# Adding the two halves of the attention result on TensorE, inside the transpose, for the first two tiles of each layer, with a new order of the whole program

## Chip, cores and metric

One core of one Trainium2 chip. The metric is the device time of one execution in microseconds. Times are medians over the runs of one kernel. Every changed kernel is compared with runs of the kernel before on the same chip in the same rounds.

## The reference

A residual stack with two identical layers over 2048 rows of 512 columns (bf16). Each layer is a linear attention with learned feature maps, then a gated MLP with ReLU gate.

```python
# per layer, 32 heads of 16
q, k, v = split(layernorm(x) @ wqkv)
phi = lambda y: concat(softmax(y @ w_phi), softmax(-(y @ w_phi)))    # 16 -> 32 features
kv, z = phi(k)^T v,  sum over rows of phi(k)
o = (phi(q) @ kv) / (phi(q) @ z + 1e-6)
x = x + o @ wo
g, u = layernorm(x) @ W_gate, layernorm(x) @ W_up      # 512 -> 1376
x = x + ((g * (g > 0)) * u) @ W_down
# twice: attention, MLP, attention, MLP
```

The keys' sums `kv` and `z` run over all 2048 rows. So all of a layer's keys must be done before any query can be used. At that point, twice in the program, TensorE has little other work, and the first tiles' attention stands alone on the way to the first MLP matmul.

## The kernel before

The rows are 16 tiles of 128. The kernel is a list of operations, each with an engine, a cost, dependencies, and a buffer pool. A planner in the kernel simulates the engines with these costs and fixes the order in which instructions are issued on each engine. Two tables steer it: `DUE`, one priority for each operation, and `PLACE`, one bit for each copy that could run on ScalarE or VectorE. Both were evidently tuned for this one program.

The softmax of `phi(q)` has two halves (`+` and `-`). Their exponentials `Eq` are multiplied by a matrix `R` (built from `kv` and `z`); numerators and denominators come out of PSUM as `N` and `DS`. VectorE makes the factors `w` and scales both halves in one multiplication to `pr`. Then the halves are added:

```python
# attend(): one tile
a = op("DVE", dve(1024, 2), ... out=pr.t[:], in0=N.t[:], in1=w...broadcast, op=Alu.mult, name="pr")
a = op("DVE", dve(512, 2), due, lambda: nc.vector.tensor_tensor(
    out=o.t[:]..., in0=pr.t[:, 0], in1=pr.t[:, 1], op=Alu.add), [a], [o], [pr], name="o", port=True)
a = turn(o, lambda: oT.t[:], how, due, a, [oT], [], "oT")
a = op("PE", mm(4, 512), ... lhsT=oT.t[:, b, :], rhs=wo[:, b, :], name="proj")        # o @ wo
a = op("DVE", dve(512), ... out=x, in0=x, in1=yp.t[:], op=Alu.add, name="resA")       # residual
# ... stats, centring (xn), turn to xnTB, then the MLP's matmuls on wgu

# turn(): a tile transposed
if how == "SP":                      # by DMA: tiles 2 to 15
    return op("SP", ... dma_start_transpose(out=dst(), in_=src.t[:]))
ps = Buf(p_b)                        # on TensorE: tiles 0 and 1 of each layer ("early")
a = op("PE", mm(4, 128), due, lambda: [nc.tensor.matmul(
    ps.t[:, b * P:(b + 1) * P], lhsT=src.t[:, b * P:(b + 1) * P], rhs=ident[:], start=True, stop=True)
    for b in range(NB)], [after, c_id], [ps], [src], name=name)
return evac(how, ...)                # copy PSUM -> SBUF, on ScalarE or VectorE as PLACE says

# the end: the order of the planner is issued; fillers on zeros go in where the plan has TensorE idle, in the start
order = arrange(ops)
for o in order:
    if o.eng == "PE": ... idle(max(0, int((o.start - free - 150) / FILL))) ...
    o.emit()
```

The softmax here doesn't subtract the row's maximum and nothing guards it: scores larger than these inputs give would overflow.

Of the kernel before, what the change touches and what calls it, by code (L numbers as in the profile page):

```python
# [10 lines left out]
H = 32  # L11
# [25 lines left out]
class Op:  # L37
# [3 lines left out]
    def __init__(self, eng, cost, due, emit, deps=(), takes=(), uses=(), name="", move=0, port=False,  # L41
                 follow=(), alt=None):
        self.eng, (self.occ, self.lat) = eng, cost
        self.due, self.emit, self.name, self.move, self.port = due, emit, name, move, int(port)
        self.deps = [d for d in deps if d is not None]
        self.follow = [d for d in follow if d is not None]
        self.takes, self.uses = list(takes), list(uses)
        self.then, self.behind, self.alt, self.twin = [], [], alt, None
# [162 lines left out]
DVE0 = (85, 170)  # L211
RLN, REXP = ((150, 265), (203, 318)), ((145, 262), (198, 315))
# [13 lines left out]
class K:  # L226
# [9 lines left out]
    "0000000100000001001000000000100000000000010001111000011000011001110000000000011010000001001111001100"  # L236
    "0100000110110100010000011011100101111100101001111000111010100001001101101100100110011001110011001001"
    "1111001110100000000011100010100100000101001110100111000101101010101000101010111001010111100010110100"
# [3 lines left out]
PHI0 = ["POOL", "POOL", "DVE"] * 5 + ["BOTH"]  # L242
PAIRN, PAIRK = 4, T
# [5 lines left out]
    76719491, 69466873, 69464194, 55720479, 42085309, 40348612, 33593703, 42085031, 50665322, 33594228, 56086954,  # L249
    58486545, 100334641, 61163217, 49431745, 41251988, 69056115, 9741064, 80414090, 80414120, 53308772, 80413780,  # L250
    106435297, 49852457, 80414139, 49848882, 56526831, 56526817, 69547873, 53741705, 49852168, 66481170, 68934086,
    55660918, 50246487, 32405931, 57594884, 55662420, 50058741, 44536605, 58281570, 3, 22509044, 49850622, 49848858,
    69548291, 69463783, 49850611, 55051722, 76716792, 0, 55324383, 47430106, 32690380, 59187722, 60929485, 45084743,
    53725584, 55713647, 55727277, 54655971, 49923445, 50246438, 55324400, 55324343, 35442704, 55802924, 35441651,
    55161101, 53685522, 51682019, 33202876, 47809082, 52941970, 53687226, 55701298, 55711066, 55655645, 44505335,
    54950229, 47610086, 55322999, 47811927, 35002194, 55588705, 62960580, 55157588, 53726567, 47768162, 55269518,
    47767416, 55571188, 53304664, 55688755, 55180830, 55625721, 50380932, 40642846, 40645264, 47809620, 55323699,
    57680173, 55268245, 54520833, 53558741, 55098763, 55683455, 55732950, 55683459, 55697315, 55770465, 52825634,
    55713412, 55710946, 55506275, 54950156, 35001190, 54949680, 34999890, 59085355, 62960363, 54948116, 55748897,
    55646532, 56083290, 53268545, 59116845, 55619542, 55763775, 53310977, 55774953, 55764998, 55740543, 52826475,  # L260
    55685321, 52784010, 55711099, 55519531, 56373630, 50382939, 52826205, 52825598, 55778163, 55771090, 55181433,
    55768958, 55684488, 55709355, 55684978, 55522442, 55648291, 55646610, 55689548, 54948629, 55098862, 47766546,
    54948487, 56010726, 55697946, 55693442, 55936025, 53268542, 44506128, 55691384, 55769572, 55545075, 55409199,
    55692897, 55662797, 55667892, 55709660, 55713749, 55700261, 55690361, 55371927, 55946741, 55947245, 55372043,
    55396376, 55760995, 55660101, 55570763, 55708913, 55708943, 50191721, 55658940, 55569634, 55658937, 55655528,
    52824974, 54566163, 55181604, 56093099, 55623488, 55927755, 55388217, 55697886, 55645404, 55667208, 55921043,
    55691484, 55685094, 55623151, 55652318, 55396329, 55703531, 55760168, 55699699, 55388529, 55623507, 55651900,
    55396324, 56045911, 55709610, 55623568, 55048436, 55709159, 56660851, 55240452, 55696214, 55974927, 55693988,
    55741153, 55693228, 55396401, 55665438, 55487833, 55388179, 55703473, 55388150, 55305368, 57292002, 55522439,
    55570606, 54081536, 55694997, 57095763, 45526601, 45175404, 54082167, 55710694, 56661198, 55697150, 54522450,  # L270
    47668141, 45175447, 49709693, 50191138, 48930643, 51185210, 41476757, 41476428, 56663182, 55710691, 55700162,
    55966393, 55623154, 55694078, 55418211, 55667889, 55662695, 50622534, 54522884, 55759099, 54522768, 55305365,
    53814510, 54207260, 51926549, 56731158, 22533505, 86923532, 49054124, 54577294, 50454445, 56663443, 26743223,
    64933030, 26742771, 41476589, 77848357, 55701636, 46564931, 86922882, 76909815, 56851302, 56665549, 49600025,
    49129654, 50619771, 50620709, 50622827, 56301309, 54209613, 56114277, 54821759, 49333488, 51487502, 52263956,
    39762113, 19221682, 41476432, 41476507, 40958443, 51486441, 50279390, 16984712, 37300570, 50960427, 49597502,
    35848215, 39760598, 24648533, 41476504, 55699989, 55704953, 48137801, 50278843, 46562185, 37300567, 49597307,
    49597499, 35844120, 55705982, 39761347, 49335617, 38759704, 49337568, 39761346, 55750849, 56154495, 33592791,
    56153063, 32405860, 51221336, 55803472, 55693594, 55803225, 55321390, 55802697, 53688156, 49597175, 49597541,
    49597913, 49596963, 58672801, 49543902, 49597043, 49596659, 55778023, 55771093, 55123240, 55776845, 55771414,  # L280
    55772175, 53557771, 53310277, 53304643, 44505573, 53310550, 55124938, 56045945, 55661057, 55711116, 55624256,
    55667825, 55396537, 56736587, 57094903, 54082104, 57408271, 54209459, 57094884, 55827685, 46563699, 56440267,
    55828521, 55702687, 46562936, 55705068, 48140907, 48140902, 56553271, 55701218, 55705063, 55720810, 56440270,
    48141651, 55702429, 55696714, 55697995, 59129153, 55703718, 55704014, 55827014, 48137480, 46562610, 30585230,
    58655341, 49560287, 21530914, 52917937, 47182136, 30584484, 55701037, 46563696, 52917833, 41444195, 41443940,
    47181589, 47181495, 41443844, 55700488, 53497782, 38496984, 56130655, 55690360, 55704606, 53137802, 55693769,
    55703325, 53137820, 55692042, 50947124, 55405040, 50987789, 41443966, 41414378, 55870566, 52917866, 55300343,
    55700485, 52129878, 61996903, 62505784, 55697736, 53137801, 55550154, 55700626, 55740601, 55699572, 55699299,
    55704914, 55699024, 58344346, 62506293, 50451565, 49470778, 53245447, 53278134, 49336219, 55704076, 55886670,
    55697360, 53497785, 55550159, 55699902, 55700360, 55698793, 55698582, 52841760, 55869605, 55108122, 54090734,  # L290
    55300268, 62506063, 62660753, 62506806, 55705573, 49344780, 55886105, 55700933, 49470866, 56146496, 55700624,
    55692773, 55692770, 55701615, 55740476, 49312541, 55752952, 49765942, 55886212, 55430767, 55238713, 55977103,
    55691820, 55688056, 47612654, 55699803, 55700555, 55697628, 55700835, 55741749, 55700975, 55702709, 55575076,
    55692884, 53991858, 53991972, 53990466, 54779534, 53853809, 54779664, 55691422, 55704463, 55620232, 55701498,
    55691964, 55738452, 55702685, 56001882, 55694740, 55702008, 55709199, 55691466, 55067255, 54761274, 56123195,
    55807312, 53991318, 53863952, 53762021, 55604349, 55704395, 55702362, 55614451, 55885531, 55702411, 55692752,
    55709972, 55702819, 56002178, 55480865, 55231139, 54147794, 57042018, 52613586, 55611316, 55693850, 55704710,
    55704869, 55540072, 55704035, 55707614, 55708907, 55702786, 55415742, 55707642, 55704187, 55610312, 55706936,
# [146 lines left out]
def kernel(  # L445
# [194 lines left out]
    def norm_A(l, tiles, dues, afters, hows):  # L640
# [9 lines left out]
        for t, due, how in zip(tiles, dues, hows):  # L650
# [3 lines left out]
                op1=Alu.mult), [a], [xn], name="xnA", port=2)  # L654
            c, i = t // C, t % C
            made.append(turn(xn, lambda c=c, i=i: xnTA[c][:, :, i * P:(i + 1) * P], how, due, b, [], [], "xnTA",
                             XPOSE if l else XPOSE_LOADS))
        return made


# [369 lines left out]
```

## Time and profile before

| | |
|---|---|
| time | 386.69 us (386.13 to 386.7, 3 runs) |
| span in the profile, granted clock | 384.4 us, 1.0 |
| matmul instructions | 2834, of them 15 fillers in the start |
| additions `o` on VectorE | 32, of them 4 on the way to a TensorE transpose |

For this study I cut the span at five starts of matmuls that can be read from the TensorE timeline: R1 and R2, the first matmul on `R` in each layer; M1 and M2, the first MLP matmul behind it; and the end. Stage 1 is R1 to M1, the middle is M1 to R2, stage 2 is R2 to M2. In the kernel before R1 is at 55.51, M1 at 65.63, R2 at 238.90, M2 at 249.40, and the end at 384.4. M1 is the start of this line of the TensorE timeline:

```profile
65.63 0.55 PE L878 MATMUL b<-xnTB,wgu 128*128 128x128 bf16 x7 [0.30 <-ACT xnTB L590]
```

The TensorE timeline of the kernel before: start, duration, engine, line, operation, tiles, size, count, then idle time and what ended it. A group starts anew where TensorE paused.

```profile
142.39 0.19 PE L723 MATMUL q<-vext,phiK 128*128 128x65 bf16 x1
142.81 0.38 PE L723 MATMUL q<-vext,phiK 128*128 128x65 bf16 x7 [0.23 <-ACT DS L590]
...
176.83 0.29 PE L723 MATMUL q<-vext,phiK 128*128 128x65 bf16 x4
177.38 0.30 PE L723 MATMUL q<-vext,phiK 128*128 128x65 bf16 x4 [0.26 <-DVE phiK L706]
```

Matmuls of 65 columns follow each other in 0.032 us when nothing stops them. From 142.39 to 142.81 there is one matmul: 0.39 us were lost, because the PSUM buffer `q` had not been emptied by ScalarE's copy of `DS`. From 176.83 to 177.38 there are four, so 0.42 us were lost, to a feature map `phiK` from VectorE.

### The profile page before, as it was taken

The page shows a single profiled execution, that of the slowest core. Times are in us where ns is not written, and L with a number is a line of the kernel's source. Part 1 is how long each engine was busy: PE and PEld are TensorE (multiplying, and loading weights), DVE is VectorE, ACT ScalarE, POOL GpSimd, SP SyncE. Part 2 cuts the span into 40 slices and gives each one's busy share as a digit, 9 for nine tenths or more (in the row PEclk, how much of TensorE's full clock was granted, in tenths as well). Part 3 has the DMA queues.
Part 4 walks back from the last instruction along what each step waited for, and adds up shares of the span by engine and source line. Part 5 has one row for each costly group of instructions (what it writes and reads, how often), then busy time and mean ns, then how long its engine had stood idle before and what let it go on. Part 6 is the DMA issues. An engine that isn't in the chain of part 4 may idle for free.

```text
span 384.4 us, 7669 instructions
## 1 busy us (share of the span) xinstructions
PE 375.9 (98%) x2834; PEld 226.1 (59%) x2834; DVE 316.6 (82%) x804; ACT 211.1 (55%) x545; POOL 40.6 (11%) x43
## 2 busy tenths in 40 slices
PE   8999998999999999999999999999999999999996
PEld 5454555877654445445666654587765445446775
DVE  6999999999999999586686688999999795565442
ACT  5999999634557215573274479955444513421431
POOL 0256720000002100050031021000000000000000
PEclk9999999999999999999999999999999999999999
DMA  8398730133222224201110000012333313002110
GB/s 226 78 232 219 176 118 2 38 69 63 41 57 55 44 41 57 55 2 34 29 35 2 15 15 1 2 32 47 79 67 81 72 23 88 0 14 77 32 31 29
DMA packets 60869, 22.83 MB, mean 59 GB/s; under 512 B 52672, under 2 KB 59808, under 8 KB 60832
## 3 DMA queue, kind: packets, MB, share of 16 engines
q1 hardware_dynamic: 60416, 21.95, 25.3%
q10 hardware_dynamic: 416, 0.39, 0.4%
q8 instruction: 22, 0.36, 0.4%
q14 instruction: 15, 0.12, 0.1%
HBM read 7.91 MB, written 2.10 MB: 26 GB/s over the span
## 4 chain that ended last, share of the span: by engine, by line
PE 84%; DVE 12%; issue 2%; ACT 1%; DVEq 0%
PE b L878 33%; PE b L911 17%; PE b L676 7%; PE b L682 7%; PE b L814 5%; PE b L764 5%; PE q L782 3%; PE b L854 3%; PE q L723 2%; DVE bstB L637 1%; DVE hT L886 1%; PE q L584 1%; DVE bstA L637 1%; DVE pr L807 1%; DVE gu L591 1%
## 5 line engine op out<-in xcount | busy, mean ns | idle before, releaser
L878 PE MATMUL b<-xnTB,wgu 128*128 128x128 bf16 (+2 forms) x1200 | 151.8, 279 | 0.3 <-ACT xnTB L590 0.3
L878 PEld LDWEIGHTS <-wgu 128*128 128x128 bf16 x1200 | 98.0, 98 | 44.1 <-issue 0.4
L911 PE MATMUL b<-wd,hT 128*128 128x512 bf16 (+2 forms) x363 | 85.9, 373 | 0.0
L882 ACT ACTIVATE gu<-b 128x512 bf16<-128x512 f32 (+1 forms) x83 | 48.4, 584 | 57.9 <-PE b L878 54.3
L706 POOL TENSOR_TENSOR phiK<-ek,sk 128x512 bf16<-128x512 bf16 x37 | 39.9, 1101 | 193.2 <-ACT sk L697 190.7
L886 DVE TENSOR_TENSOR hT<-gu 128x512 bf16<-128x512 bf16 (+1 forms) x83 | 34.8, 420 | 24.2 <-ACT gu L590 22.9
L911 PEld LDWEIGHTS <-hT 128*128 128x128 bf16 (+1 forms) x363 | 34.0, 98 | 30.8 <-DVE hT L886 0.3
L679 ACT ACTIVATE ek<-b 128x512 bf16<-128x512 f32 x64 | 35.4, 604 | 16.6 <-PE b L676 16.5
L687 DVE TENSOR_REDUCE sk<-ek 128x64 f32<-128x1024 bf16 x32 | 38.5, 1211 | 3.4 <-ACT ek L679 3.2
L768 ACT ACTIVATE Eq<-b 128x512 bf16<-128x512 f32 x64 | 36.1, 623 | 1.6 <-PE b L764 1.4
L814 PE MATMUL b<-wo,oT 128*128 128x512 bf16 x128 | 32.9, 379 | 0.5 <-ACT oT L590 0.5
L918 DVE SCALAR_TENSOR_TENSOR X<-b,rsB,X 128x512 bf16<-128x512 f32 (+1 forms) x33 | 23.6, 724 | 11.8 <-PE b L911 11.6
L590 ACT CAST gu<-b 128x512 bf16<-128x512 f32 (+1 forms) x42 | 24.4, 581 | 16.2 <-PE b L878 16.1
L590 ACT CAST N<-q 128x384 bf16<-128x384 f32 (+1 forms) x60 | 26.9, 464 | 11.3 <-PE q L782 8.5
L682 PE MATMUL b<-wv,xnTA 128*128 128x512 bf16 x128 | 32.5, 379 | 0.2 <-DVE xnTA L591 0.2
L676 PE MATMUL b<-Wk,xnTA 128*128 128x512 bf16 x128 | 32.4, 379 | 0.1
L591 DVE CAST gu<-b 128x512 bf16<-128x512 f32 (+1 forms) x41 | 26.4, 646 | 6.7 <-PE b L878 6.5
L764 PE MATMUL b<-xnTA,Wq 128*128 128x512 bf16 x128 | 31.7, 379 | 0.0
L782 PE MATMUL q<-R,Eq 128*128 128x144 bf16 x256 | 28.2, 226 | 0.7 <-DVE R L745 0.6
L782 PEld LDWEIGHTS <-Eq 128*128 128x128 bf16 x256 | 20.6, 98 | 12.8 <-issue 1.4
L818 DVE TENSOR_TENSOR X<-X,b 128x512 bf16<-128x512 bf16 x32 | 21.6, 676 | 4.2 <-PE b L814 3.9
L637 DVE BATCH_NORM_STATS2 bstA<-X 128x6 f32<-128x512 bf16 x32 | 21.3, 679 | 1.5 <-DMA X<-in_A_x_dram 1.3
(72 smaller groups left out, 390.7 us busy)
## 6 DMA issues: line engine op xcount, KB each, us to landing
out_dram<-X SPq DMA_DIRECT2D x15, 128.0 KB, 1.7
X<-in_A_x_dram SPq DMA_DIRECT2D x6, 256.0 KB, 3.3
wgu<-in_B_W_gate_dram SPq DMA_DIRECT2D x4, 344.0 KB, 3.7
wgu<-in_B_W_up_dram SPq DMA_DIRECT2D x4, 344.0 KB, 4.1
wd<-in_B_W_down_dram SPq DMA_DIRECT2D x5, 256.0 KB, 3.4
wv<-in_A_wqkv_dram SPq DMA_DIRECT2D x2, 256.0 KB, 4.3
wo<-in_A_wo_dram SPq DMA_DIRECT2D x4, 128.0 KB, 3.0
oT<-o SPq DMA_TRANSPOSE x28, 2.4
```

What stands on the lines that cost most here:

```text
L590: both = {"ACT": ("ACT", act(cols), lambda: nc.scalar.copy(out=out_(), in_=in_()), False), "DVE": ("DVE", dve(cols), lambda: nc.vector.ten ...
L676: k = op("PE", mm(4, 512), due, lambda: [nc.tensor.matmul(kp.t[:], lhsT=xnTA[c][:, b, cols], rhs=Wk2[:, b, :], start=(b == 0), stop=(b == ...
L682: v = op("PE", mm(4, 512), due_v, lambda: [nc.tensor.matmul(vp.t[:], lhsT=xnTA[c][:, b, cols], rhs=wv[:, b, :], start=(b == 0), stop=(b == ...
L687: a = op("DVE", SUM16, due, lambda: nc.vector.tensor_reduce(out=sk.t[:, row, :], in_=ek.t[:].rearrange("p g s (h f) -> p (g s h) f", f=DH) ...
L706: e.tensor_tensor(out=ph.t[:].rearrange("p g s (h f) -> p (g s h) f", f=DH)[:, lo:lo + n], in0=ek.t[:].rearrange("p g s (h f) -> p (g s h) ...
L764: q = op("PE", mm(4, 512), due(c, b), lambda b=b, qp=qp: [nc.tensor.matmul(qp.t[:], lhsT=Wq2[:, m, b * P:(b + 1) * P], rhs=xnTA[c][:, m, : ...
L782: pe.append(op("PE", mm(len(groups), GE), due, lambda ps=ps, groups=groups: [nc.tensor.matmul(ps.t[:, n * GE:(n + 1) * GE], lhsT=Eq[c][:, ...
L814: a = op("PE", mm(4, 512), due + 3, lambda: [nc.tensor.matmul(yp.t[:], lhsT=oT.t[:, b, :], rhs=wo[:, b, :], start=(b == 0), stop=(b == NB ...
L878: nc.tensor.matmul(ps.t[:, q * W:(q + 1) * W], lhsT=wgu[:, s, b, g * P:(g + 1) * P], rhs=xT.t[:, b, 0:W], start=(b == 0), stop=(b == NB - 1))
L882: nc.scalar.activation(out=gu.t[:, 0, 0:cols], in_=gp.t[:, 0:cols], func=AF.Relu)
L886: nc.vector.tensor_tensor(out=h.t[:, f0 * W:f0 * W + cols], in0=gu.t[:, 0, 0:cols], in1=gu.t[:, 1, 0:cols], op=Alu.mult)
L911: nc.tensor.matmul(yp.t[:, 0:c1 - c0], lhsT=h.t[:m, f * W + i * P:f * W + (i + 1) * P], rhs=wd[:m, f, c0:c1], start=(f == 0), stop=(f == N ...
```

## The change

For tiles 0 and 1 of each layer the addition `o` goes away. Their transpose takes `pr` in place of `o`: for each of the four blocks of 128 columns, two matmuls with the identity write to the same PSUM block, the first with `start`, the second adding. The transposed sum comes out of PSUM at no further step. The intent is to take 0.43 us of VectorE off the path to the first MLP matmul.

```diff
-        a = op("DVE", dve(512, 2), due, lambda: nc.vector.tensor_tensor(
-            out=o.t[:]..., in0=pr.t[:, 0], in1=pr.t[:, 1], op=Alu.add), [a], [o], [pr], name="o", port=True)
-        a = turn(o, lambda: oT.t[:], how, due, a, [oT], [], "oT")
+        if how == "SP" or not SUM_ON_PE:
+            o = Buf(p_o)
+            a = op("DVE", ... the same addition ...)
+            a = turn(o, lambda: oT.t[:], how, due, a, [oT], [], "oT", split=SPLIT)
+        else:
+            a = turn(pr, lambda: oT.t[:], how, due, a, [oT], [], "oT", split=SPLIT,
+                     parts=lambda: [pr.t[:, s].rearrange("p c h -> p (c h)") for s in range(2)])
@@ turn()
+                for b in range(k):
+                    for n, v in enumerate(tiles):
+                        nc.tensor.matmul(ps.t[:, b * P:(b + 1) * P], lhsT=v[:, (i * k + b) * P:(i * k + b + 1) * P],
+                                         rhs=ident[:], start=(n == 0), stop=(n == len(tiles) - 1))
@@ tables
+SUM_ON_PE, SPLIT, SUMMED = True, False, 0          # the last two are off and do nothing
-PLACE = ( ... )                                    # cut: another string of 301 bits
+PLACE = ( ... )
-DUE = ( ... )                                      # cut: another priority for each of the operations
+DUE = ( ... )
```

Both tables are new, so the order of the whole program is new: 20 copies net move from VectorE to ScalarE, three products to GpSimd, and fillers go from 15 to 12.

## The prediction

> **What bounds the kernel now.** I read the page from the top: busy time, slices, the chain that ended last.
>
> ```profile
> span 384.4 us, 7669 instructions
> PE 375.9 (98%) x2834; PEld 226.1 (59%) x2834; DVE 316.6 (82%) x804; ACT 211.1 (55%) x545; POOL 40.6 (11%) x43
> ...
> PE   8999998999999999999999999999999999999996
> ...
> PEclk9999999999999999999999999999999999999999
> ...
> PE 84%; DVE 12%; issue 2%; ACT 1%; DVEq 0%
> ```
>
> TensorE is busy 98% of the span at full clock and carries 84% of the chain. But busy matmul records overlap, so I counted the work by the spacing of starts. In the TensorE timeline four matmuls of 512 columns follow each other in 0.865 us (0.216 each), eight of 256 in 0.875 (0.109), sixteen of 128 in 0.89 (0.056), three of 144 in 0.19 (0.062), four of 192 in 0.33 (0.083), eight of 65 in 0.25 (0.032). The instruction order gives the counts: 1173, 422, 584, 256, 128 and 256. That is 253.7 + 46.1 + 32.5 + 16.0 + 10.6 + 8.2 = 367 us of real work, and 15 filler matmuls on zeros add 3.2. Of the 384.4 us of span some 14 are left: 1.3 before the first matmul, 3.2 after the last, about 3 in which the first matmuls run at half pace, and the rest is idle time between matmuls, 7 us in all. Where these idle pieces lie I read from stretches and from the timeline.
>
> ```profile
> 4.65:15.60 10.95, 10.23 (x89) 6.79 (x87) 10.23 (x23) 9.04 (x26) 0.00 (x0) 1.00 0.63 172
> 53.00:66.00 13.00, 11.09 (x95) 6.39 (x93) 11.63 (x39) 12.61 (x36) 0.00 (x0) 1.00 0.00 0
> 236.00:250.00 14.00, 13.08 (x109) 7.77 (x108) 12.40 (x39) 13.60 (x39) 0.00 (x0) 1.00 0.01 1
> 66.00:236.00 170.00, 169.52 (x1234) 101.33 (x1232) 147.20 (x357) 87.76 (x230) 17.28 (x16) 1.00 0.19 37
> 250.00:381.00 131.00, 130.94 (x1036) 83.50 (x1034) 95.14 (x274) 50.44 (x118) 0.00 (x0) 1.00 0.21 47
> ```
>
> The columns are stretch, its length, then busy time (and instructions) of TensorE, its weight loads, VectorE, ScalarE, GpSimd. TensorE is open in the start, in 53 to 66 us and a little in 236 to 250 us. The last two are the beginnings of the two attention stages: keys are done, the first two tiles' attention must pass through VectorE before the MLP has work. That is where the change is made. The TensorE timeline there:
>
> ```profile
> 58.91 0.58 PE L782 MATMUL q<-R,Eq 128*128 128x144 bf16 x6
> 60.06 0.40 PE L628 MATMUL b<-ident,o 128*128 128x128 bf16 x4 [0.57 <-DVE o L810]
> 60.30 0.59 PE L782 MATMUL q<-R,Eq 128*128 128x144 bf16 x5
> 61.14 1.04 PE L814 MATMUL b<-wo,oT 128*128 128x512 bf16 x4 [0.25 <-ACT oT L590]
> 62.01 0.29 PE L782 MATMUL q<-R,Eq 128*128 128x144 bf16 x2
> 62.53 0.40 PE L628 MATMUL b<-ident,o 128*128 128x128 bf16 x4 [0.23 <-DVE o L810]
> ```
>
> And VectorE on the same path:
>
> ```profile
> 58.85 0.69 DVE L807 TENSOR_TENSOR pr<-N,w 128x1024 bf16<-128x1024 bf16 x1
> 59.58 0.43 DVE L810 TENSOR_TENSOR o<-pr 128x512 bf16<-128x512 bf16 x1
> 59.92 0.22 DVE L798 TENSOR_TENSOR m<-DS 128x64 f32<-128x64 f32 x1
> ```
>
> The reader is to see that the transpose of o ends an idle time of TensorE (0.57 us), and that the addition o (start 59.58, end 60.01) is the link just before it. By starts, the idle pieces from 53 to 65.6 us are 0.42, 0.78, 0.53, 0.40, 0.47, 0.46: 3.1 us. In 236 to 250 us they are 0.51 and 0.71, since query projections fill the rest.
>
> **What the Trainium skill says.** "TensorE: Matmul & The Clock Gate", section "Wait — 56ns, not 53.3ns?", gives 55.6 ns from start to start for warm matmuls of 128 columns and 215.7 for 512; this trace agrees (0.056 and 0.216). Its section "Single matmul latency" has a lone matmul take (398 + N)/2.4 ns when warm, 219 ns for N = 128; the trace has exactly 219 for the four of o. So more transposes cost their spacing, not their latency. "PSUM — Partial Sum Buffer", section "The four PSUM rules", says that a matmul with the first flag overwrites and a later one without it adds: so two matmuls with an identity form the sum for nothing but their own time. No pair of this kind is in the trace yet. "Perfetto Trace Analysis", section "Identifying the Most-Contended Engine", warns that matmul busy time is a bad measure of headroom; the 98% here against 367 of 384 by spacing is that warning in small.
>
> **The change part by part.**
>
> 1. Removed: 4 of 32 additions o on VectorE (two tiles in each of two layers), 0.41 us each, 1.6 us of VectorE. VectorE isn't the bound; only those that a TensorE gap hangs on count.
>
> 2. Added: in each of the 4 transposes 8 matmuls in place of 4, so 16 x 0.056 = 0.89 us of TensorE. In the first layer (0.44 us) they fall in the 3.1 us of idle time and cost nothing. In the second they meet 1.2 us of idle time and perhaps half of 0.44 is paid: +0.2.
>
> 3. The path to the first MLP matmul. Out: 0.43 us of addition and about 0.05 of handover (pr ends at 59.54, o begins at 59.58, and the transpose begins 0.05 after its end). In: 4 x 0.056 = 0.22. Net -0.26 us per layer. In the first layer TensorE really waits for this path: -0.26. In the second it waits for it for at most 0.7 us: I take -0.1.
>
> 4. What the words do not tell: the priority table and the table that places copies on ScalarE or VectorE are new, so the order of the whole program is new. The order shows the ends of it. Fillers go from 15 to 12, all in the start, which the program puts in where its plan has TensorE idle: 3 x 0.216 = 0.65 us less idle time is planned there. The start really has 2 us to win (idle 0.58 + 0.36 + 0.26 and four fillers between 9.8 and 15.6 us), so I take -0.6. VectorE has 23 instructions fewer besides the 4 additions: ScalarE takes 20 copies net (on VectorE those of N go from 36 to 30, of its small neighbour DS as well, of 512 columns from 40 to 30, of 256 from 5 to 2, of v from 11 to 16) and GpSimd 3 products. Around the two stages the kinds of work that fill TensorE are the same (five query projections of 4 matmuls in the first, eight in the second). In the first stage tile 0's copy of oT goes from ScalarE (0.59 us) to VectorE (about 0.69), behind two small instructions of tile 1; that gives back 0.1.
>
> 5. Elsewhere, 66 to 236 and 250 to 381 us, TensorE's gaps sum to some 2 us (0.39 at 142, 0.43 at 177, 0.43 at 375 and smaller). A new order moves them at random, by perhaps 0.6 us either way. A program that has been retuned as a whole was probably kept because it gained, so I add -0.4 as a mere leaning.
>
> Sum: +0.2 - 0.26 - 0.1 - 0.6 + 0.1 - 0.4 = -1.06. Times before are 386.69, so about 385.6; rounded down a little for the relief of VectorE between 80 and 160 us (full there), 385.5.
>
> **The rivals.** (a) TensorE is the bound and pays for every added matmul: +0.89 and nothing gained, 387.4 if the new order is worth nothing. For it: 98% busy. Against it: four pieces of idle time hang on exactly these tiles. (b) The new wait takes the place of the old: pr is held longer (two buffers, freed by TensorE now, not by VectorE), so the next tile's multiplication could wait, or the copy of oT on VectorE holds up the residual addition. The two buffers are taken in turn and 1.5 us lie between two multiplications (59.54 to 61.12) while the transpose needs about 0.6, so this should not bite; if it did, +0.3, 386.9. (c) The change itself is nothing, and the retuned order is the whole result: then the gain can lie anywhere, up to 2.5 us if it closes most of the start and half the first stage, 384.2; or it can lose as much if its plan fits the chip less well than the old one did. (d) VectorE becomes free enough to let the stages between 80 and 160 us run faster: TensorE has under 0.5 us of idle time there, so the gain is below that.
>
> **Range and chances.** All idle time between matmuls is 7 us, under the 7.7 us that 2% would be, and the rest is work that the change does not remove. So faster by over 2% is all but excluded (0.01). Slower by over 2% would take a new order that opens 8 us of idle time; no instruction added comes near, and only a stage badly planned could do it (0.02). Within 2%: 0.97. The range comes from the scatter of point 5 and of the start: 383.8 to 387.2.
>
> **What would show each step.** Matmul instructions 2834 + 16 - 3 = 2847 (a few records may lack). The transposes now read pr, in eights, at about 0.45 us a group; 28 additions o are left. The idle time before the first of them in the first stage should be near what stood before o, and the first MLP matmul should start 0.2 to 0.4 us sooner, counted from the first matmul on R (10.1 us before). The key and value projections that start TensorE's closed run at 15.6 us should start near 15.0. Idle time between 66 and 236 us should still be under 2 us. The prediction is wrong if these local gains are there and the end does not move, if a gap of over 1 us opens in the middle, or if the gain is over 2.5 us, which would say that the order and not the sum was worth the most.

## The result

The changed kernel took 384.72 us (384.58 to 384.79, 4 runs), the kernel before 386.65 us (386.13 to 386.7, 4 runs) in the same rounds. The ratio is 0.9956, 95% interval 0.9941 to 0.9971: within 2%, but a real gain. Ratios here and below, with their 95% intervals, are from the fast runs of both kernels in the same rounds; they are not quite the ratio of the medians quoted (here 0.9950) or of the means (0.9953). I ran the changed kernel twice more as a control: 384.89 us (ratio 0.9969) and 385.11 us (0.9968). So a repeated run of one kernel moves by about 0.1% of the time, and differences of 0.3 us between two kernels are at the edge of what the times can tell. Spans of stages in the traces repeat far better, as the table below shows, so I argue from those and use the times as a check.

The page of the changed kernel, head and chain:

```profile
span 383.0 us, 7645 instructions
PE 373.5 (98%) x2802; PEld 226.4 (59%) x2847; DVE 307.4 (80%) x777; ACT 217.5 (57%) x565; POOL 43.5 (11%) x46
...
PE 91%; DVE 6%; issue 1%; DMA 1%; ACT 0%; DVEq 0%
```

2847 weight loads are the 2834 + 16 - 3 of the prediction; 45 matmul records are missing from this trace, so its 2802 is not a count of work. Chain shares: TensorE went from 84 to 91%, VectorE from 12 to 6%. The same five stretches as before (length, then busy time and instructions of TensorE, weight loads, VectorE, ScalarE, GpSimd, then clock, DMA share, GB/s):

```profile
4.65:15.60 10.95, 10.16 (x88) 6.59 (x88) 10.35 (x24) 10.05 (x28) 0.00 (x0) 1.00 0.61 173
53.00:66.00 13.00, 11.71 (x103) 7.06 (x102) 11.75 (x36) 11.05 (x32) 0.00 (x0) 1.00 0.00 0
236.00:250.00 14.00, 13.10 (x119) 8.41 (x119) 12.95 (x44) 11.92 (x32) 0.00 (x0) 1.00 0.00 1
66.00:236.00 170.00, 168.94 (x1218) 101.55 (x1236) 143.79 (x347) 93.44 (x246) 19.51 (x18) 1.00 0.18 37
250.00:381.00 131.00, 129.04 (x1004) 82.49 (x1017) 90.32 (x257) 54.02 (x130) 0.00 (x0) 1.00 0.22 48
```

VectorE lost 3.4 us of work in the middle stretch and ScalarE gained 5.7: that is the new placement. These sums do not tell where the time went. The five milestones do:

| us | R1 | stage 1 | middle | stage 2 | M2 to end | span |
|---|---|---|---|---|---|---|
| before | 55.51 | 10.12 | 173.27 | 10.50 | 135.00 | 384.4 |
| changed | 54.99 | 10.12 | 172.23 | 11.08 | 134.58 | 383.0 |
| difference | -0.52 | 0.00 | -1.04 | +0.58 | -0.42 | -1.4 |

The second run of the changed kernel gave stages of 10.12, 172.24, 11.07 and 135.51 us, the third 10.11, 172.24, 11.08 and 134.58. So the three columns from R1 to M2 repeat to 0.02 us and can be taken as a property of the order, unless a wait for DMA falls into one (as in e3 below). The other two move: R1 was 54.99, 54.86 and 55.09, and 54.73 to 55.45 in six more kernels that have the same order on TensorE up to there (55.36 to 55.55 in four with the old one); and the last stretch of the second run holds a wait of 0.7 us for a transpose by DMA. In the six other profiles that have the new order behind R2 unspliced it took 134.54 to 134.58, in the five with the old one 134.99 to 135.16, so this difference is one of the order too.

The second run's trace lacks no matmul, so it can be set against the kernel before by counting. Idle time here is a stretch's length less the spacing of its matmuls. The middle has the same 1254 matmuls in both, and idle time goes from 1.66 to 0.63 us: the whole -1.04. Stage 2 has 8 more identity matmuls (0.45), one query product more (0.06), and idle time goes from 0.73 to 0.80. The end has that query product less, and the two gaps before 267.51 and 296.90 us of the kernel before (0.14 and 0.22) are gone: 0.42 in all. Up to R1 idle time is 5.82 in both, and the difference of 0.65 in this run is the three fillers left out.

So in the middle the gaps are closed, with no work gone. One example: in the kernel before, eight matmuls on `phiK` at 151.13 took 0.41 us to the next start (151.54), of which 0.16 were lost. Near there the changed kernel's eight take 0.26, with nothing lost:

```profile
150.10 0.42 PE L845 MATMUL q<-vext,phiK 128*128 128x65 bf16 x8
150.36 1.89 PE L1017 MATMUL b<-xnTB,wgu 128*128 128x512 bf16 x8
```

The table is odd for a change whose subject is the two stages: stage 1 is exactly as long as before, stage 2 is longer, and all the gain lies outside them. The changed kernel's TensorE timeline in stage 1 (only the rows of the path):

```profile
54.99 0.35 PE L904 MATMUL q<-R,Eq 128*128 128x144 bf16 x3 [0.26 <-DVE R L873]
...
59.08 0.62 PE L746 MATMUL b<-ident,pr 128*128 128x128 bf16 x8
...
60.49 1.04 PE L941 MATMUL b<-wo,oT 128*128 128x512 bf16 x4
...
61.80 0.62 PE L746 MATMUL b<-ident,pr 128*128 128x128 bf16 x8 [0.15 <-DVE pr L929]
...
63.10 1.04 PE L941 MATMUL b<-wo,oT 128*128 128x512 bf16 x4
64.03 0.40 PE L746 MATMUL b<-ident,xn 128*128 128x128 bf16 x4
...
65.11 1.05 PE L1017 MATMUL b<-xnTB,wgu 128*128 128x128 bf16 x16 [0.30 <-ACT xnTB L701]
```

And its VectorE timeline:

```profile
58.33 0.69 DVE L929 TENSOR_TENSOR pr<-N,w 128x1024 bf16<-128x1024 bf16 x1
...
59.74 0.69 DVE L702 CAST oT<-b 128x512 bf16<-128x512 f32 x1
...
61.66 0.68 DVE L950 TENSOR_TENSOR X<-X,b 128x512 bf16<-128x512 bf16 x1
62.26 0.18 DVE L702 COPY DS<-q 128x32 f32<-128x32 f32 x1
62.36 0.41 DVE L702 CAST N<-q 128x256 bf16<-128x256 f32 x1
62.69 0.68 DVE L759 BATCH_NORM_STATS2 bstB<-X 128x6 f32<-128x512 bf16 x1
```

The eights on `pr` are there, and 0.75 us lie between the start of `pr` and the first of them, where 1.21 (58.85 to 60.06) lay before. So the local gain is real: 0.46 us on TensorE's first transpose, 0.31 at the residual sum (in the table below). But then VectorE does a later tile's two copies, `DS` and `N`, between the residual sum and its statistics, and the path is where it was before. In us after R1:

| link (us after R1) | before | changed | sum alone (e2) | sum taken back (e1) |
|---|---|---|---|---|
| `pr` of tile 0 starts, VectorE | 3.34 | 3.34 | 3.34 | 3.34 |
| its transpose, TensorE | 4.55 | 4.09 | 4.09 | 4.54 |
| `wo` product, TensorE | 5.63 | 5.50 | 5.59 | 5.73 |
| residual sum, VectorE | 6.98 | 6.67 | 6.66 | 7.36 |
| statistics, VectorE | 7.70 | 7.70 | 7.39 | 8.39 |
| M1 | 10.12 | 10.12 | 9.86 | 10.81 |

### The profile page after: what moved, and what is told of

Read it like the earlier page. It is cut to its first block, busy times and chain, and to the rows that moved or that the text cites. A ratio compares the mean times of both kernels' runs of the same rounds, so it can differ in the third digit from the quotient of the medians.

```text
span 383.0 us, 7645 instructions
## 1 busy us (share of the span) xinstructions
PE 373.5 (98%) x2802; PEld 226.4 (59%) x2847; DVE 307.4 (80%) x777; ACT 217.5 (57%) x565; POOL 43.5 (11%) x46
## 4 chain that ended last, share of the span: by engine, by line
PE 91%; DVE 6%; issue 1%; DMA 1%; ACT 0%; DVEq 0%
PE b L1017 36%; PE b L1050 20%; PE b L798 7%; PE b L804 7%; PE b L941 6%; PE b L886 6%; PE q L904 4%; PE b L993 3%; PE q L845 2%; DVE bstA L759 1%; DMA X<-in_A_x_dram 1%; PE b L746 1%; DVE R L867 1%; DVE pr L929 1%; DVE X L950 0%
## 5 line engine op out<-in xcount | busy, mean ns | idle before, releaser
L1050 PE MATMUL b<-wd,hT 128*128 128x512 bf16 (+2 forms) x350 | 81.9, 372 | 0.6
L828 POOL TENSOR_TENSOR phiK<-ek,sk 128x512 bf16<-128x512 bf16 x40 | 42.8, 1089 | 189.3 <-ACT sk L819 131.9
L701 ACT CAST gu<-b 128x512 bf16<-128x512 f32 (+1 forms) x55 | 31.4, 571 | 20.4 <-PE b L1017 19.0
L701 ACT CAST N<-q 128x384 bf16<-128x384 f32 (+1 forms) x66 | 29.0, 457 | 11.9 <-PE q L904 10.8
L804 PE MATMUL b<-wv,xnTA 128*128 128x512 bf16 x121 | 31.6, 379 | 0.4
L798 PE MATMUL b<-Wk,xnTA 128*128 128x512 bf16 x123 | 31.3, 379 | 0.6 <-DVE xnTA L702 0.4
L941 PE MATMUL b<-wo,oT 128*128 128x512 bf16 x120 | 31.0, 379 | 0.4
L904 PE MATMUL q<-R,Eq 128*128 128x144 bf16 x256 | 27.3, 226 | 1.5 <-DVE R L873 0.6
L702 DVE CAST gu<-b 128x512 bf16<-128x512 f32 (+1 forms) x28 | 18.7, 668 | 9.7 <-PE b L1017 9.5
(72 smaller groups left out, 385.1 us busy)
```

What stands on the lines that cost most here:

```text
L701: both = {"ACT": ("ACT", act(cols), lambda: nc.scalar.copy(out=out_(), in_=in_()), False), "DVE": ("DVE", dve(cols), lambda: nc.vector.ten ...
L798: k = op("PE", mm(4, 512), due, lambda: [nc.tensor.matmul(kp.t[:], lhsT=xnTA[c][:, b, cols], rhs=Wk2[:, b, :], start=(b == 0), stop=(b == ...
L804: v = op("PE", mm(4, 512), due_v, lambda: [nc.tensor.matmul(vp.t[:], lhsT=xnTA[c][:, b, cols], rhs=wv[:, b, :], start=(b == 0), stop=(b == ...
L828: e.tensor_tensor(out=ph.t[:].rearrange("p g s (h f) -> p (g s h) f", f=DH)[:, lo:lo + n], in0=ek.t[:].rearrange("p g s (h f) -> p (g s h) ...
L904: pe.append(op("PE", mm(len(groups), GE), due, lambda ps=ps, groups=groups: [nc.tensor.matmul(ps.t[:, n * GE:(n + 1) * GE], lhsT=Eq[c][:, ...
L941: a = op("PE", mm(4, 512), due + 3, lambda: [nc.tensor.matmul(yp.t[:], lhsT=oT.t[:, b, :], rhs=wo[:, b, :], start=(b == 0), stop=(b == NB ...
```

## The experiments

The question is which of the two parts earned the 1.4 us of span. Theory S: the sum alone. Theory O: the new order alone. Theory I: they need each other, since the new order was planned for a program without these additions. Three further questions: are the 16 added matmuls paid; what are the gaps in the middle worth; and can the two stages be had shorter? Under "Measured", the numbers behind "Stages" are R1, stage 1, the middle, stage 2, and M2 to the end, in us, from one profiled run; brackets hold the 95% interval of the ratio. All kernels gave correct results. They ran each on one chip with its own runs of the kernel before (386.42, 386.14 and 386.48 us).

### e1_sum_back: the new order, with the additions back on VectorE

```diff
   # changed kernel: directly behind pr in VectorE's queue, early tiles only; the plan doesn't see it
+  nc.vector.tensor_tensor(out=oE[t][:]..., in0=pr.t[:, 0], in1=pr.t[:, 1], op=Alu.add)
-  parts=lambda: [pr.t[:, s]... for s in range(2)]      # 8 matmuls
+  parts=lambda: [oE[t][:]]                             # 4 matmuls
```

> The changed kernel with its order of all other instructions, but the four early sums back on VectorE, each right behind its product, and four matmuls in each of the four transposes. Theory O (the new order carries the gain, the sum by itself is worth about nothing): 384.7 us, within 0.3 of the changed kernel, because the first stage gets 0.26 longer by its chain and the second gives back up to 0.44 of TensorE. Theory S (the sum on TensorE carries it): about 386.3, near the kernel before. In the trace under O: the first MLP matmul 0.2 to 0.3 us later than the changed kernel's 65.11 us, and the second stage 0.2 to 0.4 us shorter than its 11.08 us (237.34 to 248.42).

Measured: 385.8 us (385.61 to 386.4), ratio 0.9986 [0.9974, 0.9998], span 384.0. Stages: R1 54.76, 10.81, 172.24, 11.63, 134.56. The middle and the end keep the new order's gain to 0.02 us. Both stages get longer than in the changed kernel, by 0.69 and 0.55 us. The VectorE timeline:

```profile
58.82 0.42 DVE L934 TENSOR_TENSOR oE<-pr 128x512 bf16<-128x512 bf16 x1
...
61.78 0.43 DVE L934 TENSOR_TENSOR oE<-pr 128x512 bf16<-128x512 bf16 x1
62.12 0.68 DVE L954 TENSOR_TENSOR X<-X,b 128x512 bf16<-128x512 bf16 x1
```

and TensorE's:

```profile
59.30 0.40 PE L747 MATMUL b<-ident,oE 128*128 128x128 bf16 x4 [0.59 <-DVE oE L934]
```

The reader is to see that two additions lie on the path of tile 0, not one: tile 1's addition (61.78) also stands ahead of tile 0's residual sum (62.12) in VectorE's queue. Theory O as I stated it falls: in the new order the sum on VectorE costs about 1 us (1.0 by the spans, 1.24 by the two stages). One caution: the new order was made for a program without these additions, so this does not say what an order searched anew with them would reach. The order of the kernel before is one such.

### e2_sum_only: the old order, with only the sum moved

```diff
   # kernel before, old tables; the slot of o is left empty for the early tiles, the transpose reads pr
-  out=o..., in0=pr.t[:, 0], in1=pr.t[:, 1], op=Alu.add        # t < 2 only
+  turn(..., parts=lambda: [pr.t[:, s]... for s in range(2)])  # 8 matmuls in place of 4
```

> The kernel before with its own order, and only the four early sums moved into the transposes on TensorE. Theory O: 386.6 us, within 0.4 of the kernel before (first stage -0.26, second stage about +0.3). Theory S: 384.9 to 385.3, most of the measured gain of 1.7 to 1.9 us. In the trace under O: the transposed copy of the first tile starts about 0.25 us sooner after the product than before, and the three gaps of TensorE at 142, 151 and 177 us are still there (about 0.97 us in sum).

Measured: 386.19 us (385.82 to 386.93), ratio 0.9997 [0.9985, 1.001], span 384.4. Stages: R1 55.55, 9.86, 173.27, 10.65, 135.07. Stage 1 is 0.26 us shorter, which is the prediction's -0.26 to the digit. Stage 2 is 0.15 longer, and the whole is not to be told from the kernel before. Theory S falls. Where the freed VectorE time went shows in its own waits:

```profile
243.25 0.23 DVE L803 TENSOR_TENSOR m<-DS 128x64 f32<-128x64 f32 x1 [0.52 <-ACT DS L590]
...
243.97 0.69 DVE L591 CAST oT<-b 128x512 bf16<-128x512 f32 x1 [0.27 <-PE b L633]
```

VectorE comes to the next tile sooner and finds `DS` not yet copied by ScalarE: 0.52 us of waiting in stage 2, where 0.43 us of addition were taken out. The transpose itself is held by its place in TensorE's queue: it starts 4.64 us after R2 in both kernels (before 243.54 - 238.90; here 243.32 - 238.68), because a query projection and three query products stand in front without a pause. So in the old order tile 0's own addition is off the path of stage 2. Tile 1's was on it: before, it stood between tile 0's residual sum and its statistics (6.98, 7.59 and 7.92 us after R2). Here the residual sum comes 0.22 later (7.20), behind a transpose that is four matmuls longer, and the statistics at 7.92 again: what the one removal gave, the added matmuls took. The 0.15 comes after that: tile 1's `wo` product, behind tile 0's second transpose, waits 0.13 us for ScalarE's copy of tile 1's `oT`, where it waited for nothing before.

With the kernel before and the changed one, these two make a square of spans: 384.4 (neither), 384.4 (sum), 384.0 (order), 383.0 (both). The two together gain 1.4 us, where the separate gains add to 0.4. But R1 is in these spans, and it moves from run to run. Counted from R1 on, the order alone is 0.35 us slower than the kernel before (+0.69, -1.03, +1.13, -0.44), the sum alone 0.04 faster, and both together 0.88 faster. Theory I stands, by the stages; the ratios alone (0.9986 for the order, 0.9956 to 0.9969 for both) have intervals that overlap.

### e3_pairs_twice: the added matmuls doubled

```diff
-  for b in range(k):
+  for b in [b for b in range(k) for _ in range(2 if name == "oT" else 1)]:   # changed kernel; each pair issued twice
```

> The changed kernel with the eight matmuls of each early transpose issued twice (16; the second pass overwrites the first, the result is the same): 32 matmuls more, 1.78 us of TensorE by their spacing. If TensorE pays for all of it: 386.5 us. If the first stage has room for the second tile's (0.44) and the rest is paid, by the chain of the first tile (0.44) and in the second stage (0.89): about 386.0. If the idle time takes it all: 384.8.

Measured: 387.12 us (386.93 to 387.46), ratio 1.0018 [1.0006, 1.003], span 385.1. Stages: R1 54.73, 10.93, 172.98, 11.92, 134.54. Each transpose now holds TensorE 0.90 us (first to next start, 58.82 to 59.72) in place of 0.45, so 0.90 were added in each stage; stage 1 grew by 0.81, stage 2 by 0.84. The added matmuls are paid nearly in full in both stages of the new order; they do not fall into idle time. A further 0.75 came in the middle. A wait of a `wo` product for a transpose by DMA accounts for it (0.6 in the view, 0.73 by the spacing before 76.34 us). From the list of waits of e3 (who waited for what: total us, times, longest):

```profile
PE b L941 <- DMA oT<-o: 0.6, 1, 0.6
```

The changed kernel's second run shows a like wait (0.7 us, after M2; its span was 383.8), with no change at all. So this part of e3 may be scatter of the DMA, not a cost of the matmuls. It is not shown: all five runs of e3 took at least as long as the profiled one (386.93).

### after_again, after_third: controls

```diff
   # none to the program: the changed kernel, first with its order given as a fixed list, then as it is
```

> A control: the changed kernel again, its order written out as a list in place of the table (the instructions of every engine are the same, in the same order). 384.7 us, ratio 0.9956 within 0.001. If it gives less of a gain, the first measurement was lucky.

> A control: the changed kernel once more, on the chip of the three runs beside it. Nothing new is expected: 384.7 to 384.9 us, ratio to the kernel before 0.996 to 0.997.

Measured: 384.89 us (384.51 to 385.58), ratio 0.9969 [0.9956, 0.9983], and 385.11 us (384.57 to 385.89), ratio 0.9968 [0.9953, 0.9983]. The gain is real (no interval reaches 1), and in these two nearer to 0.3 than to 0.44%. The fixed list is a fair carrier for the experiments that splice orders.

### h_start_new, g_middle_new, g_stages_old, g_stages_old_sum_back: orders spliced

These carry the sum on TensorE (the last one on VectorE) and take one stretch of the program from the new order and the rest from the old, or the reverse.

```diff
   # the list of operations in order, cut at R1, M1, R2, M2
   # h_start_new:            new | old | old | old | old
   # g_middle_new:           old | old | new | old | old
   # g_stages_old:           new | old | new | old | new
   # g_stages_old_sum_back:  the same, with the addition on VectorE for the early tiles
```

> The sum on TensorE throughout; the order of instructions from the new table up to the end of the first key stage, from the old table after that. By the two traces the new start is worth 0.5 us by the first matmul on R (54.99 against 55.51 us). Theory O with additive stages: 0.5 us below the run with the old order and the sum on TensorE, so about 386.1 us if that gives 386.6. If the start is hidden by a later wait: no change.

> The sum on TensorE; the order from the new table only between the first MLP matmul and the first matmul on R of the second layer, the old order elsewhere. By the traces this stretch is 172.23 us in the new order and 173.27 in the old, and the three gaps of TensorE in the old one sum to 0.97. Theory O (each stretch of order carries its own gain): 385.2 us, 1.0 below the run with the old order and the sum on TensorE (386.2); the gaps at 142, 151 and 177 us gone. If the gap moves to a later stage: no change, 386.2.

> The sum on TensorE; new order for start, middle and end, old order for the two attention stages, which are shorter in it with the sum on TensorE (9.86 and 10.65 us against 10.12 and 11.08). If stretches add up: 0.7 below the changed kernel, 384.0 us, faster than both. If the new stages are longer because they do work that the end then lacks: no change, 384.7.

> As the run with the old order in the two attention stages and the new one elsewhere, but the four early sums back on VectorE. Theory I (what the sum is worth hangs on the order around it: in the old stages VectorE only waits for a copy of ScalarE in its place): within 0.3 us of that run, about 384.2, and below the changed kernel although the sum is on VectorE. Theory S' (the sum is worth 1.1 us wherever the rest of the order is new): 385.1.

Measured: h_start_new 385.92 us (385.44 to 386.09), ratio 0.9984 [0.9972, 0.9996], R1 at 55.40. That lies within the 54.73 to 55.45 of other kernels with this start, so it does not say that the start is worth less alone: the run of matmuls without a pause begins at 14.89 us as in the changed kernel (14.86, before 15.60). g_middle_new 386.94 us (386.54 to 387.48), ratio 1.0019 [1.0006, 1.0033]. g_stages_old 388.22 us (387.79 to 388.51, fast runs), ratio 1.005 [1.0037, 1.0064]; its profiled run fell in a slow state (495.33 us at a granted clock of 0.755), so its trace is not used. g_stages_old_sum_back 388.37 us (388.11 to 388.51), ratio 1.0055 [1.0042, 1.0068].

The last three missed what I expected, and the fault was in the experiment. TensorE around M1 in g_middle_new:

```profile
65.71 0.35 PE L902 MATMUL q<-R,Eq 128*128 128x144 bf16 x3 [0.80 <-ACT N L699]
66.78 0.35 PE L902 MATMUL q<-R,Eq 128*128 128x144 bf16 x3 [0.72 <-ACT DS L699]
66.97 1.22 PE L1015 MATMUL b<-xnTB,wgu 128*128 128x128 bf16 x19
```

The two orders have different query products behind them at M1. At the seam those left over from one order had to be put in front of the first MLP matmul, where each waits for a copy to free its PSUM buffer. M1 came 1.75 us later than in e2 (11.61 us after R1 in place of 9.86). So these runs do not measure what a stretch is worth. One reading survives: the middle of g_middle_new took 172.50 and that of g_stages_old_sum_back 172.20, against 173.27 in the old order, but the six query products put in front of M1 (0.37 us by their spacing) are work that left the middle. So 0.40 and 0.70 are left of the 1.04: a part of the middle's gain goes with its order, whatever stages stand around it.

### r1_gaps_closed: the two gaps in the middle, alone

The old order with the sum on TensorE (e2), and two groups of `kv` products one group later in TensorE's queue.

```diff
-wd,hT x7 | vext,phiK x8 | wd,hT x3 | vext,phiK x16
+wd,hT x10 | vext,phiK x24
 ...
-wd,hT x4 | vext,phiK x8 | wd,hT x8
+wd,hT x12 | vext,phiK x8
```

> The old order with the sum on TensorE (as in e2_sum_only, 386.19 us), and one more thing: two groups of eight products of keys and values, those at whose heads TensorE waited 0.39 us at 142.4 and 0.42 us at 176.8, stand one group of MLP matmuls later in TensorE's queue. Theory 'the gain in the middle is these waits': both gaps go, the second attention stage starts some 0.8 us sooner (first matmul on R at about 237.9 in place of 238.68), and the total is about 385.4, a ratio of 0.9978. Rival 'the work between is bound by more than these two waits' (VectorE, 80 to 100% busy there, sets the pace): the gaps open again within a few us, and the total stays at 386.2, ratio 0.9995.

Measured: 385.68 us (385.24 to 386.56), ratio 0.9984 [0.9969, 0.9998], span 383.9. Stages: R1 55.39, 9.86, 172.84, 10.65, 135.16. TensorE's timeline:

```profile
142.65 0.93 PE L843 MATMUL q<-vext,phiK 128*128 128x65 bf16 x24
...
150.37 0.50 PE L843 MATMUL q<-vext,phiK 128*128 128x65 bf16 x8
151.16 2.75 PE L1015 MATMUL b<-xnTB,wgu 128*128 128x512 bf16 x11 [0.29 <-DVE X L948]
```

Both gaps are gone (24 products run in one piece). The first one's 0.39 us came back 8 us later: the MLP matmul at 151.16 waits for VectorE, 0.54 us beyond the pace, where e2 has 0.16 there. Both are 85.91 us after M1. The second one's 0.42 us was kept: the middle is 0.43 us shorter, and that reached the end, since stage 2 and the last stretch are within 0.1 us of e2's. (The times differ by 0.5 us, but on different chips, with intervals that overlap, and R1 came 0.16 sooner.) So each theory was right about one gap. A gap is worth its length only if what comes next on TensorE does not wait for an engine that has not moved.

### r2_stage1: the copies moved from the path of stage 1

The changed kernel, with the two copies on VectorE shown above moved behind the normalized tile, and two groups of three query products moved behind the first MLP group on TensorE (the text counts only one of the two).

```diff
 VectorE: X<-X,b
-DS<-q | N<-q | bn_stats | bn_aggr | xn
+bn_stats | bn_aggr | xn | DS<-q | N<-q
 TensorE:
-q<-R,Eq x6 | wo,oT x4 | ident,xn x4 | q<-R,Eq x6 | xnTB,wgu x16 | q<-R,Eq x3
+q<-R,Eq x3 | wo,oT x4 | ident,xn x4 | q<-R,Eq x3 | xnTB,wgu x16 | q<-R,Eq x9
```

> The changed kernel, with copies of DS and N of a later tile moved on VectorE from ahead of the first tile's statistics to behind the normalized tile, and on TensorE three of the six query projections behind them moved behind the first MLP group. Theory 'the gain of the first stage was given back to these copies': the first MLP matmul comes some 0.35 us sooner, 9.8 us after the first matmul on R in place of 10.12, and the total is about 384.4, ratio 0.996 or under. Rival 'the query projections fill this wait anyway': what was moved has to be done later, a new gap behind the first MLP group takes the 0.35 us back, and the total stays at 384.8.

Measured: 385.64 us (385.46 to 386.42), ratio 0.9983 [0.997, 0.9996], span 384.6: slower than the changed kernel beside it (385.11), by 0.5 us in the medians, which the intervals do not tell apart, and by 1.14 in the stretches from R1 on. Stages: R1 55.45, 10.04, 173.48, 11.08, 134.55. TensorE's timeline:

```profile
63.55 1.04 PE L939 MATMUL b<-wo,oT 128*128 128x512 bf16 x4 [0.49 <-ACT oT L699]
64.43 0.39 PE L744 MATMUL b<-ident,xn 128*128 128x128 bf16 x4
...
67.63 0.35 PE L902 MATMUL q<-R,Eq 128*128 128x144 bf16 x3 [0.71 <-ACT DS L699]
```

The statistics did start 0.32 us sooner (62.83 - 55.45 = 7.38 us after R1, 7.70 in the changed kernel), and the normalized tile too. But its transpose stands behind tile 1's `wo` product in TensorE's queue, and that one waited for tile 1's `oT` until 63.55; the transpose went 0.06 us sooner than in the changed kernel (8.98 after R1 against 9.04). Stage 1 gained 0.08. Then the query products that I had moved waited behind the first MLP group for a copy of `DS`: 0.71 us in the view, 0.88 by spacing (66.38 to 67.63 less six times 0.062). With the 0.37 us of the six themselves that is 1.25, and the middle grew by 1.25. The rival was right, and more than right: the copies were not what bound stage 1 alone. Two waits of about the same length lay side by side.

### r3_stages: the same, and stage 2

```diff
 (r2, and:)
 VectorE: X<-X,b
-oT<-b (tile 1)
 ScalarE: Eq x3
+oT<-b (tile 1)
 ... N, DS copies ... Eq x1, and two Eq behind a later copy
```

> As r2_stage1, and in the second attention stage the copy of oT of tile 1 goes from VectorE to ScalarE, and two exponentials that stand in its way there move back. Theory 'in the second stage the gain was given back to this copy (0.68 us on VectorE between the residual sum and its statistics)': the stage takes some 10.6 us in place of 11.08, and the total is 0.4 to 0.5 under r2_stage1, about 383.9, ratio 0.995. Rival 'TensorE is full there, and the stage is as long as its work': the stage keeps 11.0 us and the total is that of r2_stage1.

Measured: 386.2 us (385.82 to 386.72), ratio 0.9994 [0.9981, 1.0007], span 384.0. Stages: R1 54.88, 10.04, 173.49, 11.03, 134.56. By its stages it should take as long as r2; by its median it took 0.56 us longer and by its span 0.6 less (an R1 that came sooner). Nothing follows from those. Stage 2 gained 0.05 us where I expected 0.5. TensorE before M2:

```profile
249.14 0.35 PE L902 MATMUL q<-R,Eq 128*128 128x144 bf16 x3 [0.49 <-ACT DS L699]
249.44 0.50 PE L991 MATMUL b<-wgu,xnTB 128*128 128x192 bf16 x4
```

The same wait of 0.49 us for ScalarE's copy of `DS` stands before M2 in the changed kernel too (at 248.08). But it does not set M2: the three query products take 0.19 us, and M2 came 0.11 later still here, 0.15 in the changed kernel. For M2 in the changed kernel (line 993) the trace names the wait: VectorE's copy `xnTB`, the last link of tile 0's path. What held that path lies before it. The move did bring tile 0's statistics 0.49 us sooner (7.92 after R2, 8.41 in the changed kernel) and the normalized tile 0.15, yet its transpose began 9.85 us after R2 against 9.86, since tile 1's `wo` product and six query products stand in front of it on TensorE without a pause. The theory of the `oT` copy falls. The rival stands in part: up to that transpose TensorE is full, but 0.65 us of idle time follow it.

None of the experiments beats the changed kernel.

## Why the prediction was right or wrong

The predicted time, 385.5 us, and its range hold the result (384.72, then 384.89 and 385.11). The sum was -1.06; the spans show -1.4. Its terms were not as good as the sum, and that it came so near is in part luck: the two stages were forecast at -0.06 together and came out at +0.58, the stretches elsewhere at -0.4 and came out at -1.46, and these errors have opposite signs.

- **Part 1 and the counts** (4 additions out, 16 matmuls in, 3 fillers out): as predicted, 28 additions left, 2847 weight loads.
- **Part 2, the added matmuls.** 0.056 us each is right (0.45 for a group of 8 in the changed kernel, 0.90 for 16 in e3). Stage 2 was under-sized: "perhaps half of 0.44 is paid: +0.2". e3 shows them paid nearly whole (0.84 of 0.90). Stage 2 got longer by 0.58: by the counts above 0.45 of added matmuls, 0.06 of one more query product and 0.07 of idle time. In stage 1 "cost nothing" was wrong too in the new order: e3 added 0.81 of 0.90 there (tile 0's half of it is the delay that part 3 counts). In the old order, for which it was worked out, the forecast was near: parts 2 and 3 give +0.1 for stage 2, e2 shows +0.15. The 219 ns of a lone matmul, which the prediction calls a match with the skill, is no check: matmul ends are modelled in these traces.
- **Part 3, the path.** -0.26 in stage 1 was exact where nothing else changed (e2: 10.12 to 9.86). In stage 2 the -0.1 did not come: tile 0's transpose stood behind a query projection, and what tile 1's addition gave, the longer transpose took. In the changed kernel stage 1 shows 0.00, so the prediction's own sign for this step, a first MLP matmul 0.2 to 0.4 us sooner after R1, failed there.
- **Part 4, stage 1 in the new order.** I gave back 0.1 for the copy of `oT` on VectorE. What was given back is 0.26, and in another place: between the residual sum and the statistics stand two copies of a later tile. r2 shows that TensorE's queue would have held the path there anyway. Rival (b), a new wait in place of the old, is what happened in stage 1, though not by `pr`'s buffers, as I had it. In stage 2 TensorE had no room up to the normalized tile's transpose (see r3).
- **Part 4, the start.** -0.6 predicted, about -0.5 seen at R1 (54.86 to 55.09 in three runs against 55.51). With all kernels of each start it is 54.73 to 55.45 against 55.36 to 55.55, so the size is loose.
- **Part 5, elsewhere.** This is the term that was mis-sized: "-0.4 as a mere leaning", with "some 2 us" of gaps moved "at random". Middle and end gave -1.04 and -0.42. Three gaps of the old order in the middle (in the groups at 142.39, 151.13 and 176.83; 0.39, 0.16 and 0.42 us, together 0.97) are absent from the new one, which accounts for nearly all of the -1.04. The gap of 0.43 at 375 us that the prediction lists never was: four of the twelve matmuls there have 512 columns, not 256, and they fill it (8 x 0.109 + 4 x 0.216 = 1.74, from 375.41 to 377.15). "At random" was the wrong idea, if the new order was kept because it was faster; no run shows how it was made.
- **Rival (c)**, that the new order is the whole result: half right, and this is the point that neither I nor the rival put properly. The order alone is worth 0.4 us of span (e1), all of it at R1, the sum alone nothing (e2), both 1.4. The new order's gains in the middle and end (1.46) are there with the sum on either engine, but in its stages the additions lie on the path, and e1 pays 1.24 us for them.
- **Rival (a)** (+0.89, every matmul paid) was right on the matmuls, but not on the total.

What stays open: what an order searched anew for the sum on VectorE would reach, and which entries of the two tables closed the gaps of the middle. r1 shows that one of them can be closed by hand for 0.43 us.

## What to carry to other kernels

When a small change comes with a new schedule, separate them before crediting either: run the change in the old order, and the new order with the change undone. An addition removed from an engine's queue gains only where the next engine's queue is not held by something else; read each queue's next entry and its wait before you count the gain. Cut the span at a few named instructions: here the three stretches from R1 to M2 repeated to 0.02 us from run to run while whole times scattered by 0.3 us and more. Then count the instructions in each stretch, so that work that crossed a border is not taken for a gain.

## What the Trainium skill lacked or had wrong

- "TensorE: Matmul & The Clock Gate", section "Back-to-back issue gap", gives 81 ns (N = 128) and 131 ns (N = 512) per matmul for a real stream of weight loads and matmuls, and says that the N/2.4 + 2.5 form is wrong there by as much. In this kernel, which is such a stream with one weight load per matmul, the traces show 0.056 and 0.216 us from start to start: that form (55.8 and 215.8 ns) holds here, and the two other figures do not.
- "Perfetto Trace Analysis", section "Optimizing Scalar/DVE Operations", gives an overhead of about 125 ns for each VectorE instruction on PSUM, as engine-busy time, and about twice that in the profiled latency. In the changed kernel VectorE's copies from PSUM took 0.33 us for 256 columns (62.36 to the next start at 62.69) and 0.60 for 512 (245.15 to 245.75). From these two, 1.05 ns a column, the fixed part is about 0.06 us. By the records' own lengths (0.41 and 0.68 us) it is 0.14. Each is about half of the page's.
- No page of the skill says what a sum inside a transpose costs. Here eight identity matmuls of 128 columns in pairs that accumulate hold TensorE 0.45 us, as much as eight that do not (0.056 us each), and 16 hold it 0.90; the addition of 512 columns that they replace took 0.43 us on VectorE.
